# A retention layer and two feed-forward layers on one core: a new order for the opening, and every later step planned anew

## The chip, the cores and the metric

The kernel runs on one core of one Trainium2 chip. A core has a matrix engine (TensorE, "PE" in the profile; its weight loads are "PEld"), a vector engine (VectorE, "DVE"), a scalar engine (ScalarE, "ACT"), a general engine (GpSimd, "POOL") and a queue engine that here only starts transfers (SyncE, "SP"). Each engine works through its own instructions in the order in which they were written and waits on semaphores for the others. The metric is the device time of one execution in microseconds (us); lower is better.

## What is computed

The inputs are float32 for q, k and v (2 batches, 8 heads, 768 steps, 64 features a head) and 64-bit for the four weight matrices.

```python
for t in range(S):                       # retention, gamma = 1 - 2**(-5-h) by head
    state = gamma * state + einsum('bhd,bhe->bhde', k[:, :, t], v[:, :, t])
    y[:, :, t] = scale * einsum('bhd,bhde->bhe', q[:, :, t], state)
x = y as (1536 tokens, 512)
h = x @ moe_w_in                         # 512 -> 2048
g = where(h > 0, h, exp(min(h, 0)) - 1)  # ELU
x = g @ moe_w_out                        # 2048 -> 512
h = x @ moe2_w_in
g = max(h, 0) + log1p(exp(-abs(h)))      # softplus
out = g @ moe2_w_out
```

## The kernel before

**Steps.** The work is cut into some 1,950 small steps, each with a short name and up to three numbers. A table of such names, written out in the kernel (`TABLE`), is walked through from left to right once, while the program is built; each step appends its few instructions to the engines' queues. So the table alone sets the order of every engine's instructions and of the transfers. Tiles and PSUM banks are handed out in the same order, and an instruction waits until the last user of its tile is done.

**Retention.** The 1536 tokens are 12 chunks of 128, `j` = 0 to 11 (0 to 5 are the first batch, 6 to 11 the second). A chunk needs its transfers `Lq.j`, `Lk.j`, `Lv.j` (line 180 up to chunk 5, lines 183 to 188 after; from chunk 8 on q and k come in a second, blocked form by eight steps `Lb`, four small transfers each, line 204), one table of decay factors for each batch (`Lg.0`, `Lg.1`, line 771), transposes on TensorE (`Tq`, `Tk`, line 370) and their copies out of PSUM (`tq` on DVE, `tk` on ACT, lines 387 to 391; from chunk 8 on both are transposes on DVE, line 377), the scores (`S`, PE line 437), their causal mask (`m`, DVE line 447), the state (`dv` on POOL, line 363; `ST` on PE, line 417; `st` on DVE, lines 426 to 429; `sp` on POOL, line 402), and the product with the values (`O`, PE lines 459 to 480). The result, the layer's x, is split into two tiles whose sum carries the precision: the rounded part (`xh`, ACT line 495) and the rest (`xl`, DVE line 499).

**First feed-forward layer.** It goes over 48 units, `u` = 0 to 47: 3 blocks of 512 tokens (four chunks) by 16 slices of 128 of the 2048 hidden features. `H.u` is the hidden product (12 matmuls, PE line 517), `ar`, `ae` (ACT lines 525, 528) and `ab` (DVE line 532) are the ELU, `gh` (ACT line 536) and `gl` (DVE line 541) its two halves, `R.u` is the product that returns to 512 features (12 matmuls, PE line 558). `ih`, `il` and `oh`, `ol` split the weight slices of the unit in the same way (ACT line 300, DVE line 306). Unit 0 needs chunks 0 to 3. The hidden product's PSUM bank is one of two in turn, and in the second batch the state product `ST` borrows the one that is free.

**Weights.** `Lw.i` loads one weight slice of 512 KB (line 269); numbers 0 to 31 are the first layer's, 32 to 63 the second's. There are four buffers, and a fifth while the retention lasts. Four steps turn the 64-bit numbers of a slice into float32: `ct.i` and `cl.i` on ACT (lines 274, 279), `cj.i` and `cs.i` on DVE (lines 284, 293); `cs` frees the buffer.

**Second feed-forward layer.** After `R.47` the second layer runs on the finished tokens (`M`, PE line 696; `Q`, PE line 751), with its own splits (`bh`, `bl`, `sh`, `sl`, `wh`, `wl`); the finished sums of the first layer leave PSUM in steps `F` (ACT line 585, DVE line 587), and `u.0` to `u.2` are copies of partial sums that the products wait for (ACT line 703).

**What sets the order.** All q, k, v and weight transfers are issued from SP in the table's order, on one queue. `kc` are matmuls on zeros ahead of and between the first real ones.

```python
    for t in TABLE.split():
        name, *args = t.split(".")
        steps[name](*map(int, args))
```

Of the kernel before, what the change touches and what calls it, by code (L numbers as in the profile page):

```python
# [27 lines left out]
ct.3 cs.2 cl.3 cj.3 S.4 ar.0 Lw.7 cs.3 ih.2 H.1 ae.0 il.2 Lw.8 oh.0 m.4 ct.4 dv.5 cl.4 ab.0 ol.0 Tq.5 gh.0 O.4 cj.4 Lq.7
ar.1 gl.0 ae.1 cs.4 ct.5 H.2 cl.5 ab.1 ih.3 tq.5 xh.4 il.3 gh.1 cj.5 Lb.64 ct.6 xl.4 R.0 cl.6 cs.5 ar.2 gl.1 Lw.9 ct.7 oh.1
cj.6 ae.2 ol.1 H.3 cl.7 Lw.11 cs.6 ct.8 ab.2 ih.4 cj.7 cl.8 Lb.65 il.4 gh.2 cs.7 Tk.5 ST.4 ar.3 gl.2 Lk.6 tk.5 R.1 cj.8 oh.2  # L30
st.4 ct.9 Lw.10 cl.9 ol.2 sp.5 Lw.14 ae.3 cj.9 Lv.6 ct.11 ab.3 S.5 cs.9 gh.3 Lk.7 cs.8 oh.3 H.4 gl.3 ih.5 ol.3 cl.11 Lw.12
m.5 ct.10 cl.10 R.2 il.5 Lw.13 ar.4 cj.10 ae.4 cj.11 dv.6 cs.10 ab.4 Lb.66 ih.6 R.3 cs.11 gh.4 il.6 oh.4 Lw.16 gl.4 Lw.15
# [20 lines left out]
st.10 gl.24 H.25 oh.24 ol.24 R.23 ar.25 ih.27 ae.25 il.27 ab.25 H.26 gh.25 oh.25 gl.25 ol.25 R.24 ar.26 ih.28 ae.26 il.28
ab.26 H.27 gh.26 oh.26 gl.26 ol.26 S.11 ar.27 ih.29 R.25 ae.27 il.29 m.11 ab.27 H.28 gh.27 oh.27 gl.27 ol.27 O.11 end yh.0.0
ar.28 yl.0.0 ih.30 ae.28 il.30 yh.0.1 ab.28 R.26 xh.11 yl.0.1 gh.28 xl.11 gl.28 H.29 oh.28 ol.28 R.27 ar.29 ih.31 ae.29
il.31 ab.29 H.30 gh.29 oh.29 gl.29 ol.29 R.28 ar.30 ih.32 ae.30 il.32 ab.30 cs.32 H.31 gh.30 oh.30 Lw.36 gl.30 cl.34 ol.30
cj.34 R.29 ar.31 ih.33 ae.31 il.33 ab.31 ct.36 cs.33 H.32 gh.31 oh.31 cw.0.0 Lw.37 gl.31 cl.35 ol.31 cw.0.1 cw.0.2 R.30
# [773 lines left out]
```

## Time and profile before

| | |
|---|---|
| median of 3 runs | 584.48 us (583.4 to 585.72) |
| the profiled execution's own time | 584.83 us |
| its span, first to last instruction | 583.1 us |
| mean granted TensorE clock | 0.993 |
| busy: PE, PEld, DVE, ACT, POOL | 570.0, 485.5, 451.5, 371.7, 28.4 us |
| HBM traffic | 44.58 MB read, 3.15 MB written |

The span is what the trace covers; 1.73 us of the execution's own time lie around it. "Busy" counts an engine's computing instructions only. TensorE's granted clock is 1.0 at 2.4 GHz and 0.5 at 1.2 GHz.

### The profile page before, as it was taken

The numbers are of one execution on the slowest core, as the hardware profiler recorded it, in microseconds if no ns is written. First come the engines' busy times: TensorE is split into PE (matmuls) and PEld (weight loads), VectorE is DVE, ScalarE is ACT, GpSimd is POOL, SyncE is SP. The second block draws the span as 40 slices with busy tenths as digits, with TensorE's granted clock in tenths as the row PEclk, the third lists the DMA queues.
The fourth block names the chain that finished last, engine by engine and source line by source line (L and its number), as shares of the span: only waits on it lengthen the run. The fifth ranks groups of instructions, "written<-read, shape, count | busy, mean of one in ns | idle before, by whom it ended". The sixth has DMA issues, their size and how long they took to land.

```text
span 583.1 us, 8690 instructions
## 1 busy us (share of the span) xinstructions
PE 570.0 (98%) x3236; PEld 485.5 (83%) x3236; DVE 451.5 (77%) x785; ACT 371.7 (64%) x678; POOL 28.4 (5%) x37
## 2 busy tenths in 40 slices
PE   8899999999979999999999999999999999999997
PEld 5788888888857888888888899889999989998995
DVE  4799899976465465999999899877788876666653
ACT  2488988845544555888999785555567655555442
POOL 3312102101010000000000000000000000000000
PEclk9999999999979999999999999999999999999999
DMA  9998687523510000314677000000000200000002
GB/s 200 245 311 212 183 264 206 143 43 60 161 38 1 2 1 36 104 42 150 210 239 232 2 0 1 1 1 2 0 1 0 110 2 0 2 0 1 0 1 108
DMA packets 75833, 48.28 MB, mean 83 GB/s; under 512 B 53520, under 2 KB 69904, under 8 KB 75792
## 3 DMA queue, kind: packets, MB, share of 16 engines
q1 hardware_dynamic: 75504, 47.46, 29.5%
q8 instruction: 25, 0.41, 0.3%
q10 hardware_dynamic: 288, 0.28, 0.1%
q14 instruction: 16, 0.13, 0.1%
HBM read 44.58 MB, written 3.15 MB: 82 GB/s over the span
## 4 chain that ended last, share of the span: by engine, by line
PE 91%; SPq 3%; DMA 3%; ACT 1%; DVE 1%; issue 0%; DVEq 0%; ACTq 0%
PE psb L517 23%; PE psb L751 22%; PE psb L558 22%; PE psb L696 20%; DMA raw<-moe_w_in 3%; SPq L180 2%; PE psb L437 1%; SPq L269 1%; PE psb L466 1%; PE psb L370 0%; PE psb L417 0%; PE psb L459 0%; PE psb L480 0%; DMA out_dram<-o 0%; PE psb L474 0%
## 5 line engine op out<-in xcount | busy, mean ns | idle before, releaser
L751 PE MATMUL psb<-wo,g 128*128 128x512 f32 x576 | 142.1, 392 | 0.0
L751 PEld LDWEIGHTS psb<-wo,g 128*128 128x128 f32 x576 | 107.5, 188 | 19.5
L517 PE MATMUL psb<-x,wh 128*128 128x512 f32 x384 | 97.8, 397 | 5.6 <-DVE st L428 3.6
L517 PEld LDWEIGHTS psb<-x,wh 128*128 128x128 f32 x384 | 72.4, 191 | 22.0 <-ACT gh L536 4.0
L696 PE MATMUL psb<-op,wx 128*128 128x384 f32 x336 | 67.0, 339 | 0.0
L696 PEld LDWEIGHTS psb<-op,wx 128*128 128x128 f32 x336 | 60.2, 188 | 2.5
L306 DVE TENSOR_TENSOR wl<-wi,wh 128x512 fp32r<-128x512 f32 x48 | 33.7, 701 | 33.6 <-ACT wh L300 33.6
L721 ACT ACTIVATE hx<-hx 128x384 f32<-128x384 f32 x64 | 33.2, 520 | 37.5 <-DVE hx L717 37.4
L558 PE MATMUL psb<-gh,wh 128*128 128x512 f32 x192 | 56.4, 400 | 0.0
L558 PE MATMUL psb<-gh,wl 128*128 128x512 f32 x192 | 54.4, 390 | 0.0
L558 PE MATMUL psb<-gl,wh 128*128 128x512 f32 x192 | 54.3, 389 | 0.0
L517 PE MATMUL psb<-x,wl 128*128 128x512 f32 x192 | 52.2, 394 | 0.0
L284 DVE SCALAR_TENSOR_TENSOR cl<-cm,cl 128x512 int32<-128x512 int32 x64 | 45.2, 710 | 8.4 <-ACT cl L279 8.4
L274 ACT ACTIVATE cm<-raw 128x512 f32<-128x512 f32 x64 | 42.8, 668 | 12.0 <-DMA raw<-moe_w_in 8.0
L525 ACT ACTIVATE e<-psb 128x512 f32<-128x512 f32 x48 | 28.4, 592 | 34.4 <-PE psb L517 34.3
L536 ACT ACTIVATE gh<-e 128x512 fp32r<-128x512 f32 x48 | 30.2, 629 | 24.3 <-DVE e L532 24.3
L731 ACT ACTIVATE g<-hx 128x384 fp32r<-128x384 f32 x64 | 33.2, 520 | 18.7 <-DVE hx L725 18.6
L669 DVE TENSOR_TENSOR wo<-wo,wo 128x512 fp32r<-128x512 f32 x32 | 22.0, 687 | 29.7 <-ACT wo L665 29.7
L517 PEld LDWEIGHTS psb<-x,wl 128*128 128x128 f32 x192 | 36.6, 191 | 7.8
L279 ACT ACTIVATE cl<-raw 128x512 int32<-128x512 uint32 x64 | 42.5, 665 | 0.6 <-DVE wo L293 0.5
L558 PEld LDWEIGHTS psb<-gh,wl 128*128 128x128 f32 x192 | 36.1, 188 | 7.7
L558 PEld LDWEIGHTS psb<-gl,wh 128*128 128x128 f32 x192 | 36.0, 188 | 7.5
(102 smaller groups left out, 890.9 us busy)
## 6 DMA issues: line engine op xcount, KB each, us to landing
raw<-moe_w_in SPq DMA_DIRECT2D x32, 512.0 KB, 4.8
raw<-moe_w_out SPq DMA_DIRECT2D x32, 512.0 KB, 4.3
out_dram<-o SPq DMA_DIRECT2D x11, 256.0 KB, 2.2
early<-q SPq DMA_DIRECT2D x4, 256.0 KB, 5.0
early<-k SPq DMA_DIRECT2D x4, 256.0 KB, 4.9
early_v<-v SPq DMA_DIRECT2D x4, 256.0 KB, 5.3
qb<-q SPq DMA_DIRECT2D x64, 16.0 KB, 2.0
qb<-k SPq DMA_DIRECT2D x64, 16.0 KB, 1.8
```

The costliest lines, as they stand in the source:

```text
L274: nc.scalar.activation(out=m, in_=raws[i][:, :, :, 1].bitcast(F32), func=AF.Copy, scale=2.0 ** -112)
L279: nc.scalar.activation(out=l, in_=raws[i][:, :, :, 0].bitcast(U32), func=AF.Copy, scale=2.0 ** -29 * (1 - 2.0 ** -12), bias=-0.499)
L284: nc.vector.scalar_tensor_tensor(out=l, in0=m.bitcast(I32), scalar=3, in1=l, op0=ALU.logical_shift_left, op1=ALU.bitwise_or)
L306: nc.vector.tensor_tensor(out=l, in0=wf[f][o], in1=ws[u, o][0].bitcast(F32), op=ALU.subtract)
L517: nc.tensor.matmul(b, w[:, kk, :], x[:, kk, :], start=(n == 0), stop=(n == len(seq) - 1))
L525: nc.scalar.activation(out=e, in_=hb[u], func=AF.Relu, scale=-1.0)
L536: nc.scalar.activation(out=gh, in_=acts[u], func=AF.Copy)
L558: nc.tensor.matmul(acc[i], st[:, i * P:(i + 1) * P], mv, start=(fresh and p == 0), stop=(f == NF - 1 and p == 2))
L696: nc.tensor.matmul(bank_p[b], w[:, h, k], x[l][:, k], start=(start and i == 0), stop=(i == len(seq) - 1), skip_group_check=True)
L721: nc.scalar.activation(out=e, in_=e, func=AF.Softplus)
L731: nc.scalar.activation(out=t[:, 0], in_=hid[Q, c][1], func=AF.Copy)
L751: nc.tensor.matmul(sums2[s], t[:, x, i * P:(i + 1) * P], o[:, w], start=(left[s] == 0 and p == 0), stop=(left[s] == 2 * NQ - 1 and p == 2) ...
```

## The change

The table is replaced, and nothing else. Both tables hold the same steps, each exactly once. Up to `R.0`, the first product that returns to 512 features, the order is now one written out by hand; everything after it comes from a new run of the planner that made the old table, with measured times for the issue of transfers in its costs.

```diff
 TABLE = """
 ST.5 ST.11 sp.7 st.5 sp.6 sp.8 Tq.8 Tk.8 sp.9 Tq.9 Tk.9 sp.10 Tq.10 Tk.10 sp.11 Tq.11 Tk.11 st.11 Lq.0 Lk.0 Lk.1 Lq.1 Lv.0
-Lv.1 Lk.2 Lq.3 Lq.2 dq.0 Tq.0 kc.3 Lg.0 tq.0 Tk.0 Lv.2 Tk.1 tk.0 tk.1 S.0 Lk.3 dq.1 Lv.3 Tq.1 dv.0 m.0 kc.2 ST.0 Lw.0 dv.1
...
+Lg.0 Lv.1 Lk.2 dq.0 Lq.3 Tq.0 kc.3 Lq.2 tq.0 Tk.0 Lv.2 Tk.1 tk.0 tk.1 S.0 Lw.0 dq.1 Lk.3 Tq.1 dv.0 kc.2 tq.1 Lk.4 m.0 ST.0
...
```

TensorE's order is the same to the last step. Of the steps on SP, ACT, DVE and POOL, 57 of 130, 259 of 676, 225 of 764 and 8 of 21 stand at another place in their engine's queue. Three places matter below.

The first is ScalarE's queue in the opening, after `tk.2`. Before, it reads `xh.1 tk.3 ct.0 cl.0 xh.2 ih.0 tk.4 ct.1 cl.1 ct.2 cl.2 xh.3` (line 495 is `xh`, 387 `tk`, 274 and 279 a weight slice's `ct` and `cl`, 300 `ih`):

```order
L495 ACTIVATE x_234<-psb 128x4x128
L387 ACTIVATE early_v<-psb 128x512
L274 ACTIVATE cm<-raw 128x512
L279 ACTIVATE cl<-raw 128x512
L495 ACTIVATE x_234<-psb 128x4x128
L300 ACTIVATE wh<-wi_116 128x512
L387 ACTIVATE kT<-psb 128x512
L274 ACTIVATE cm<-raw 128x512
L279 ACTIVATE cl<-raw 128x512
L274 ACTIVATE cm<-raw 128x512
L279 ACTIVATE cl<-raw 128x512
L495 ACTIVATE x_234<-psb 128x4x128
```

Now the same stretch of the queue reads `ct.0 cl.0 xh.1 tk.3 xh.2 ih.0 ct.1 cl.1 xh.3 tk.4 ih.1 ct.2`:

```order
L274 ACTIVATE cm<-raw 128x512
L279 ACTIVATE cl<-raw 128x512
L495 ACTIVATE x_235<-psb 128x4x128
L387 ACTIVATE early_v<-psb 128x512
L495 ACTIVATE x_235<-psb 128x4x128
L300 ACTIVATE wh<-wi_116 128x512
L274 ACTIVATE cm<-raw 128x512
L279 ACTIVATE cl<-raw 128x512
L495 ACTIVATE x_235<-psb 128x4x128
L387 ACTIVATE kT<-psb 128x512
L300 ACTIVATE wh<-wi_116 128x512
L274 ACTIVATE cm<-raw 128x512
```

`xh.3`, the last line 495 of each, moved ahead of `ct.2`; `ct.0` moved ahead of `xh.1`. Beside it, DVE has `tq.1` ahead of `m.0` and `m.3` ahead of `xl.2` now, POOL has `sp.1` ahead of `dv.1` and `sp.3` ahead of `dv.3`, and SP issues `Lg.0` four transfers earlier (ahead of `Lv.1`), `Lw.0` ahead of `Lk.3` and `Lv.3`, and `Lw.3` and `Lw.4` ahead of `Lv.4`.

The second place is SP's queue at the end of the retention's transfers. Before, the first four weight slices of the second layer stand behind the last blocked transfers (line 204) and ahead of `Lv.11` (lines 183 to 186, v) and `Lk.11` (k):

```order
L204 DMA qb<-k 32x4x32 x16
L269 DMA raw<-moe_w_in 128x4x256 x4
L183 DMA v<-v 128x4x64
L185 DMA v<-v 64x4x64
L186 DMA v<-v 64x4x64
L183 DMA k<-k 128x4x64
L185 DMA k<-k 64x4x64
L186 DMA k<-k 64x4x64
```

Now:

```order
L204 DMA qb<-k 32x4x32 x16
L183 DMA v<-v 128x4x64
L185 DMA v<-v 64x4x64
L186 DMA v<-v 64x4x64
L269 DMA raw<-moe_w_in 128x4x256 x2
L183 DMA k<-k 128x4x64
L185 DMA k<-k 64x4x64
L186 DMA k<-k 64x4x64
L269 DMA raw<-moe_w_in 128x4x256 x2
```

`Lw.32` and `Lw.33` moved behind `Lv.11`, `Lw.34` and `Lw.35` behind `Lk.11` too.

The third place is ScalarE's queue where these four slices are taken up. Before, from `ar.19` on (lines 525, 528 and 536 are the ELU of a unit):

```order
L525 ACTIVATE e<-psb 128x512
L300 ACTIVATE wh<-wi_118 128x512
L528 ACTIVATE e<-e 128x512
L274 ACTIVATE cm<-raw 128x512
L279 ACTIVATE cl<-raw 128x512
L274 ACTIVATE cm<-raw 128x512
L279 ACTIVATE cl<-raw 128x512
L300 ACTIVATE wh<-wo_127 128x512
L536 ACTIVATE gh<-e 128x512
L274 ACTIVATE cm<-raw 128x512 x2
L525 ACTIVATE e<-psb 128x512
```

Now `ar.19` is followed by `ih.21 ae.19 gh.19 oh.19 ar.20` and no line 274; the four `ct` stand two units later. From `oh.21` on:

```order
L300 ACTIVATE wh<-wo_129 128x512
L274 ACTIVATE cm<-raw 128x512
L279 ACTIVATE cl<-raw 128x512
L274 ACTIVATE cm<-raw 128x512
L279 ACTIVATE cl<-raw 128x512
L525 ACTIVATE e<-psb 128x512
L300 ACTIVATE wh<-wi_120 128x512
L528 ACTIVATE e<-e 128x512
L274 ACTIVATE cm<-raw 128x512
L300 ACTIVATE wh<-wo_130 128x512
L536 ACTIVATE gh<-e 128x512
L274 ACTIVATE cm<-raw 128x512
```

`ct.32` moved from the middle of unit 19's ELU to behind unit 21's.

At the passage from the first layer to the second the last conversions come later: on ACT `cl.62`, `ct.63` and `cl.63` now stand behind `u.0`, and on DVE `cj.61`, `cs.61`, `cj.62` and `cs.62` behind `gl.47`; before, only `cj.63` and `cs.63` did.

## Rows read from the trace of the kernel before

**Rows 1.** Groups by line: busy, mean ns | idle before them, what ended it.

```profile
L517 PE MATMUL psb<-x,wh 128*128 128x512 f32 x384 | 97.8, 397 | 5.6 <-DVE st L428 3.6 <-ACT x L495 1.9
```

**Rows 2.** Busy time by engine in stretches of the span, with granted clock and DMA.

```profile
0.00:20.00 20.00, 17.50 (x188) 12.76 (x188) 10.81 (x20) 4.87 (x7) 8.21 (x19) 1.00 1.06 209
20.00:40.00 20.00, 17.31 (x158) 14.16 (x157) 16.91 (x28) 14.15 (x25) 4.51 (x6) 1.00 1.06 288
...
160.00:180.00 20.00, 16.38 (x60) 12.99 (x59) 11.43 (x17) 9.64 (x18) 2.45 (x2) 0.83 0.13 29
```

**Rows 3.** The same view of three short stretches around the long stall.

```profile
162.38:166.00 3.62, 0.00 (x1) 0.03 (x1) 2.33 (x5) 3.27 (x7) 0.38 (x1) 0.89 0.35 79
166.00:171.46 5.46, 5.46 (x13) 4.30 (x14) 3.83 (x4) 0.11 (x1) 2.08 (x2) 0.50 0.00 0
171.46:174.50 3.04, 3.04 (x13) 2.49 (x13) 1.29 (x2) 2.17 (x4) 0.00 (x0) 0.91 0.00 0
```

**Rows 4.** Timeline, 145 to 176 us: start, duration, instruction, [idle before it <-releaser].

```profile
144.78 7.49 SPq L204 DMA_DIRECT2D qb<-k  x16
...
152.36 2.04 SPq L269 DMA_DIRECT2D raw<-moe_w_in  x4
...
156.70 0.66 ACT L274 ACTIVATE cm<-raw 128x512 f32<-128x512 f32 x1 [4.26 <-DMA raw<-moe_w_in]
...
159.51 0.37 SPq L183 DMA_DIRECT2D v<-v  x1
...
161.93 0.66 ACT L274 ACTIVATE cm<-raw 128x512 f32<-128x512 f32 x1 [0.86 <-DMA raw<-moe_w_in]
162.50 0.58 ACT L525 ACTIVATE e<-psb 128x512 f32<-128x512 f32 x1
...
166.00 3.75 PE L517 MATMUL psb<-x,wh 128*128 128x512 f32 x8 [3.62 <-DVE st L428]
```

**Rows 5.** Timeline of the opening, 18 to 30 us.

```profile
18.39 1.04 POOL L363 TENSOR_TENSOR early_v<-early_v,dec 128x512 f32<-128x512 f32 x1 [0.66 <-DMA early_v<-v]
...
18.70 0.66 PE L370 MATMUL psb<-ident,early 128*128 128x128 f32 x4
...
20.50 0.67 ACT L274 ACTIVATE cm<-raw 128x512 f32<-128x512 f32 x1 [0.51 <-DMA raw<-moe_w_in]
...
21.20 1.16 PE L437 MATMUL psb<-early_v 64*128 64x128 f32 x16
...
23.70 1.28 DVE L447 TENSOR_TENSOR A<-psb,mask 128x512 f32<-128x512 f32 x2
...
25.04 0.98 PE L480 MATMUL psb<-A,early_v 128*64 128x128 f32 x13 [0.17 <-DVE A L447]
...
26.52 0.66 PE L370 MATMUL psb<-ident,q 128*128 128x128 f32 x4
...
27.36 0.66 ACT L274 ACTIVATE cm<-raw 128x512 f32<-128x512 f32 x1 [1.66 <-DMA raw<-moe_w_in]
...
28.47 0.59 ACT L495 ACTIVATE x<-psb 128x512 fp32r<-128x512 f32 x1
...
29.11 1.20 PE L517 MATMUL psb<-x,wh 128*128 128x512 f32 x4 [1.93 <-ACT x L495]
```

**Rows 6.** Timeline of VectorE and TensorE, 119 to 124 us.

```profile
119.09 0.64 DVE L306 TENSOR_TENSOR wl<-wi,wh 128x512 fp32r<-128x512 f32 x1
...
122.47 1.98 PE L517 MATMUL psb<-x,wh 128*128 128x512 f32 x8
```

**Rows 7.** Timeline at the passage to the second layer, 326 to 334 us.

```profile
326.20 1.06 ACT L647 ACTIVATE wx<-wi 128x1024 fp32r<-128x1024 f32 x1 [1.36 <-DVE wi L637]
...
329.14 0.56 DVE L725 SCALAR_TENSOR_TENSOR hx<-hx 128x384 f32<-128x384 f32 x1 [0.61 <-ACT hx L721]
...
330.53 1.04 ACT L585 ACTIVATE y<-psb 128x384 f32<-128x384 f32 x2 [1.05 <-DVE y L587]
...
333.19 0.29 DVE L587 COPY y<-psb 128x128 f32<-128x128 f32 x1 [1.46 <-PE psb L558]
```

More of the change, by code (lines that the diff above doesn't have):

```diff
@@ L28 @@
[L28 to L32, printed above, removed]
@@ L53 @@
[L53 to L57, printed above, removed]
@@ L115 @@
[L115 to L117 removed]
+Lg.0 Lv.1 Lk.2 dq.0 Lq.3 Tq.0 kc.3 Lq.2 tq.0 Tk.0 Lv.2 Tk.1 tk.0 tk.1 S.0 Lw.0 dq.1 Lk.3 Tq.1 dv.0 kc.2 tq.1 Lk.4 m.0 ST.0
+Lv.3 st.0 O.0 sp.1 Lw.1 S.1 xh.0 dv.1 Lq.4 xl.0 Tk.2 m.1 ST.1 tk.2 Lw.2 Tq.3 Tq.2 st.1 O.1 Lw.3 dv.2 tq.2 tq.3 sp.2 S.2 Lw.4
@@ new lines @@
+H.21 oh.20 Lw.33 Lk.11 ol.20 R.19 Lw.34 dv.11 ar.21 Lw.35 ih.23 ae.21 il.23 ab.21 H.22 gh.21 oh.21 gl.21 ct.32 ol.21 cl.32
+ct.33 cj.32 R.20 cl.33 ar.22 cj.33 ih.24 ae.22 il.24 ab.22 ct.34 H.23 oh.22 gh.22 ol.22 ct.35 gl.22 S.10 ar.23 ih.25 R.21
+ae.23 il.25 m.10 ab.23 H.24 gh.23 oh.23 gl.23 ol.23 O.10 ar.24 ih.26 ae.24 il.26 ab.24 ST.10 xh.10 gh.24 R.22 xl.10 st.10
+gl.24 H.25 oh.24 ol.24 R.23 ar.25 ih.27 ae.25 il.27 ab.25 H.26 gh.25 oh.25 gl.25 ol.25 R.24 ar.26 ih.28 ae.26 il.28 ab.26
+H.27 gh.26 oh.26 gl.26 ol.26 S.11 ar.27 ih.29 R.25 ae.27 il.29 m.11 ab.27 H.28 gh.27 oh.27 gl.27 ol.27 O.11 end yh.0.0 ar.28
@@ new lines @@
+Q.0.0 j.0.3 vh.0.2 j.0.1 wh.2 c.1.0 vh.0.3 wl.1 vh.0.1 M.1.6 yh.1.0 vl.0.2 vl.0.1 yh.1.1 M.1.5 cw.2.0 cw.2.1 u.1 cw.2.2
+Q.0.1 vl.0.3 bh.2 n.1.0 wl.2 s.1.0 bl.2 M.1.7 wh.3 j.1.0 Q.0.2 cw.2.3 u.2 wl.3 vh.1.0 sh.2 c.1.2 vl.1.0 M.1.4 n.1.2 sl.2
+s.1.2 M.1.3 j.1.2 c.1.3 cw.3.0 vh.1.2 n.1.3 Q.0.3 cw.3.1 s.1.3 c.1.1 j.1.3 n.1.1 vh.1.3 vl.1.2 M.2.1 s.1.1 cw.3.2 wh.4
+vl.1.3 j.1.1 bh.3 M.2.2 wl.4 u.0 Q.1.0 bl.3 vh.1.1 c.2.0 vl.1.1 M.2.6 n.2.0 cw.3.3 s.2.0 yl.1.0 sh.3 M.2.5 j.2.0 u.1 sl.3
+Q.1.1 vh.2.0 vl.2.0 cw.4.0 cw.4.1 cw.4.2 M.2.7 wh.5 yl.1.1 Q.1.2 wl.5 u.2 cw.4.3 c.2.2 xt.1.0 M.2.4 n.2.2 xt.1.2 s.2.2 M.2.3
@@ new lines @@
+u.0 vh.9.1 vl.9.3 Q.9.0 c.10.0 vl.9.1 n.10.0 sl.11 s.10.0 M.10.6 j.10.0 cw.12.1 vh.10.0 M.10.5 cw.12.0 u.1 vl.10.0 Q.9.1
+M.10.7 wh.21 wl.21 Q.9.2 u.2 c.10.2 n.10.2 s.10.2 M.10.4 j.10.2 M.10.3 vh.10.2 c.10.3 vl.10.2 bh.12 Q.9.3 n.10.3 c.10.1
+s.10.3 n.10.1 bl.12 sh.12 s.10.1 M.11.1 j.10.3 wh.22 j.10.1 vh.10.3 M.11.2 wl.22 u.0 vh.10.1 vl.10.3 Q.10.0 c.11.0 vl.10.1
+n.11.0 sl.12 s.11.0 M.11.6 j.11.0 cw.13.1 vh.11.0 M.11.5 cw.13.0 u.1 vl.11.0 Q.10.1 M.11.7 wh.23 wl.23 Q.10.2 u.2 c.11.2
+n.11.2 s.11.2 M.11.4 j.11.2 M.11.3 vh.11.2 c.11.3 vl.11.2 bh.13 Q.10.3 n.11.3 c.11.1 s.11.3 n.11.1 bl.13 sh.13 s.11.1 M.12.1
@@ L118 @@
+n.15.1 j.15.3 s.15.1 vh.15.3 j.15.1 Q.15.0 vl.15.3 vh.15.1 vl.15.1 Q.15.2 Q.15.3 Q.15.1 o.1.1 o.1.0 o.1.2 d.1.0 d.1.1 d.1.2
+o.1.3 d.1.3 o.1.4 d.1.4 o.1.5 d.1.5
 """
```

158 lines of the change are left out of this document (75 added, 83 removed).

## The prediction

> **What bounds the kernel now.** I read the groups by line first, for the product that opens each unit, then the busy time by stretches, then the timelines around the stretches where TensorE is not full. TensorE's own work is untouched by the change: its order is the same to the last step, so only what it waits for can move. The hidden product's 384 matmuls stood idle 5.6 us in all, and two waits make that up: 3.6 us for a step of the state on VectorE and 1.9 us for x on ScalarE [rows 1]. By stretches TensorE is short of full in the first 40 us (17.50 and 17.31 of 20) and around 160 to 180 us (16.38, at a mean granted clock of 0.83) [rows 2]. The two waits lie in the second and third of these.
>
> The long one runs from 162.38 to 166.00 us, and it costs more than its length [rows 3]. `H.21` and `R.19`, 24 matmuls, follow it. The first 12 take 5.46 us at a granted clock of 0.50 (1.2 GHz) and the other 12 take 3.04 us; twelve at the full clock take 2.72 us, which is half of 5.46 to 0.01. So the stall is worth 3.62 idle, 2.74 and 0.32 of slow clock: **6.68 us**.
>
> Where it comes from stands in the timeline [rows 4]. SP needs 7.49 us for 16 small blocked transfers, 0.47 us each, and so starts `Lw.32` to `Lw.35` only at 152.36. ScalarE stands at `ct.32`, in the middle of unit 19's ELU, for 4.26 us until 156.70, and once more until `Lw.35` has landed (161.93). Only then, at 162.50, does it reach `ar.20`, the first step of the next unit's ELU. VectorE's `ab.20`, its transpose for chunk 11 and `st.9` queue behind that, and `st.9` holds the PSUM bank that `H.21` needs.
>
> The short wait is in the opening [rows 5]. TensorE has done `Tq.4` at 27.18 (26.52 and 0.66) and stands until 29.11 for `xh.3`. The product that `xh.3` copies, `O.3`, ended at 26.02 (25.04 and 0.98). But ScalarE's queue had `ct.2` first, which waited 1.66 us for `Lw.2`, began at 27.36, and let `xh.3` begin at 28.47.
>
> **The change, part by part.** *The long stall.* The four `ct` now stand behind `oh.21`, and the loads behind `Lv.11` and `Lk.11`. `Lv.11` takes the buffers of chunk 9, so SP cannot start it before `ST.9` is done: SP stood from 154.40 (152.36 and 2.04) to 159.51 for that [rows 4]. With the opening's 1.93 us (below) taken off, that is 157.6. Its three issues at 0.47 end at 159.0, so `Lw.32` lands at 159.0 and the 4.34 us that it took before (152.36 to 156.70): 163.3. `Lw.35` follows two weight issues and three more for `Lk.11`; the four loads landed 1.74 us apart before ((161.93 - 156.70)/3), three of these gaps and 0.8 us for `Lk.11`, an estimate at under half of a load, give 169.4. ScalarE needs them when unit 21's ELU is through: `R.18` ends at 162.38 - 1.93 = 160.45, `H.21` 2.72 us later at 163.2, and six steps in a chain at 0.58 to 0.66 us [rows 4, 6] bring it to `ct.32` at 167.0 and to `ct.35`, behind the next unit's `ar` and `ae`, at about 171. The loads are there 3.7 and 1.6 us ahead, and what stands behind a late `ct.35`, the ELU of unit 23, has most of a unit (two products, 5.44 us) in hand. I take the whole **-6.68 us**; the bounds are nothing, if ScalarE meets the same wait in a later unit, and 6.68.
>
> The Trainium skill speaks against this part: "DMA: Bandwidth & Descriptors", section "Issuing engines are not separate DMA queues", has it that the time to start a transfer is usually small beside the transfer. The trace does not agree for these: 16 issues held SP for 7.49 us [rows 4]. By the page a plan that counts issue times has nothing to gain here, and the sum would keep the 6.68 us.
>
> The Trainium skill's "TensorE: Matmul & The Clock Gate", section "Terms", puts the price of a slow clock at the throttled time by the share of the clock that is missing. The clocks of rows 3 make 6.8 us at 0.50, so 3.4 us by that rule; the matmuls show 2.74 and 0.32, 3.06 us, since part of the slow time falls on an idle engine. The sum by the rule would be 0.3 us lower.
>
> *The opening, from `xh.3` on.* With `ct.2` behind it, `xh.3` follows `O.3` at once, and `ct.1`, which stands ahead of it, finds `Lw.1` landed two transfers before `Lw.2`. The end of `O.3` at 26.02 and 0.59 for `xh.3` is 26.6, under `Tq.4`'s end at 27.18: `H.0` starts then, **-1.93 us**. Had TensorE nothing between `O.3` and `H.0`, `xh.3` itself would be 2.42 us earlier (28.47 - 26.05), which bounds the gain.
>
> *The opening, ahead of `O.3`.* Two moves cost something there. `tq.1` ahead of `m.0` puts the mask one step later on VectorE, 0.64 us (1.28/2 [rows 5]), and TensorE's `O.0`, `S.1`, `O.1`, `S.2` with it, 0.5 us as there was little room. `Lw.0` ahead of `Lk.3` delays that by one weight load, 2.11 us (20.50 - 18.39, behind `Lv.3`). `Lk.3` stood one transfer ahead of `Lv.3`; an estimate of half a load's time between them puts it at 17.3 before and 19.4 now, so `Tk.3` moves from 18.70 to 19.5 at the least, `S.3` from 21.20 to about 22.3, ending at 23.5. But before, `m.3` began only at 23.70, 1.3 us after `S.3` had ended (21.20 and 1.16), for it stood behind `xl.2` and two conversions; now it stands ahead of `xl.2` and begins at 23.5 to 23.7. So `O.3` ends where it did: **0**, bounds -0.2 and +1.0. What is late next if `S.3` slips further is `m.3` one for one. `dv.3`, whose `Lv.3` now lands behind `Lw.0` and `Lk.4` (2.11 and, by the same estimate, 1.05), begins at 21.6 instead of 18.39, or at about 23 behind `sp.3`, ends by 24.1 and is hidden behind `m.3`, whose second half ends at 24.9; without that cover it would cost its own 1.04. The same for `ct.0` ahead of `xh.1`: it ties `xh.1`, `xl.1`, `st.2` and `sp.3` to `Lw.0`, and `m.3` covers them up to a landing of about 19.5 (I expect 18.4 to 18.7, two transfers ahead of the 20.50 of before).
>
> *The long middle.* TensorE arrives 1.93 us earlier at every unit, and the other engines must keep up. The smallest lead that I find of a split weight on its product is `H.15`'s, 119.73 (119.09 and 0.64) against 122.47: 2.7 us, and that half is wanted only in the product's last third [rows 6]. The new plan has the conversions there one step later on both engines, with fewer ahead of each split. I take **0**, bounds 0 and +1.
>
> *The passage to the second layer.* Three conversions more on ScalarE, 0.56 us apart, 1.7 us, meet idle times of 1.36 and 1.05; four more on VectorE, 0.6 apart, 2.4 us, meet 0.61 and 1.46 that are shown [rows 7]. I take **+0.3**; with the cover gone it would be 2.4 on VectorE, where `F.47` and the partial sum behind it (333.19) would come late and `M.0.3` after them.
>
> Sum against the profiled execution's own 584.83: - 6.68 - 1.93 + 0 + 0 + 0.30 = 576.52. The median of the runs is 0.35 lower (584.48), so **576.2 us**.
>
> **Rivals.** *The stall stays.* The loads are not started earlier than before (159.0 against 152.36), so if ScalarE still meets them unlanded, two units on, the same queue stands behind it. For it: the four loads still come last on SP and need up to 9.6 us to land (152.36 to 161.93). Against: 3.7 us of room. Only the opening is gained then: 582.9, or 584 with the opening lost too; I take 582 to 586. It is also what the Trainium skill's rule on issue times, above, would give. *The opening gives nothing.* `Lk.3`, `ct.0` and `dv.3` are all tied to `Lw.0`; if it lands later than 19.5, `O.3` and `H.0` slip one for one. At 21.4 the gain is gone: 578.1, up to 581 with the passage's whole cost. *Slower.* The place is SP at `Lv.11`: whatever delays `ST.9` or the blocked transfers ahead now delays all four weight loads too, which before did not wait for it. From a landing of `Lw.35` past some 176 us (171 and most of a unit) each us costs one, and an idle TensorE costs the 3.06 us of slow clock again. To be slower than 587.4 it must land past 176 + 8.2 + 2.9 - 3.1 = 184, 15 us later than I expect; SP had nothing of that size in it before.
>
> **How the numbers follow.** Half a per cent, 2.9 us, is about what a measurement of this kernel can tell from no change. My forecast holds with 0.70, between 574.5 and 578; the opening without gain has 0.12 (578 to 581); the stall that stays 0.09 (582 to 586); slower 0.05; better than 574.5, by a wait that I have not seen, 0.04. Faster: 0.70 + 0.12 + 0.04 = 0.86; same 0.09; slower 0.05. Range 574.5 to 580.5: forecast and most of the second case, about 0.8.
>
> **What would show it.** In the profile after: the groups by line of the hidden product with hardly any idle time behind VectorE and ScalarE; a granted clock of 1.0 from 160 to 180 us; `H.0` at 27.2; `ct.32` without a wait; `M.0.3` no more than 0.3 us later against `R.47`. Wrong would be a new wait of ScalarE or VectorE for a transfer between 40 and 180 us, or a `Tk.3` past 20 us.

## The result

| | before | changed |
|---|---|---|
| median of the timed runs | 585.1 us (four runs, 583.4 to 586.14) | **579.33 us** (four runs, 578.8 to 580.23) |
| the profiled execution's own time, span | 584.83, 583.1 | 578.8, 576.7 |
| mean granted clock | 0.993 | 1.000 |

The ratio is 0.9906, with a 95 % interval of 0.9877 to 0.9934: faster by 0.9 %, as forecast in sign, and 3.1 us short of the forecast 576.2. The page's groups by line and the busy time by stretches answer to [rows 1] and [rows 2]:

```profile
L517 PE MATMUL psb<-x,wh 128*128 128x512 f32 x384 | 96.0, 392 | 1.2 <-DVE st L428 1.2
...
L558 PE MATMUL psb<-gh,wl 128*128 128x512 f32 x192 | 54.5, 390 | 0.8 <-DVE wl L306 0.8
```

```profile
core 0: us, PE busy (x) PEld busy (x) DVE busy (x) ACT busy (x) POOL busy (x), PEclk, DMA share, GB/s
0.00:20.00 20.00, 17.45 (x176) 12.31 (x176) 9.31 (x16) 5.28 (x8) 7.16 (x18) 1.00 1.09 211
20.00:40.00 20.00, 19.60 (x177) 16.33 (x173) 19.65 (x33) 15.34 (x28) 5.85 (x7) 1.00 1.02 283
160.00:180.00 20.00, 20.00 (x100) 16.35 (x99) 13.38 (x22) 11.74 (x22) 2.40 (x2) 1.00 0.50 132
```

The two waits of the hidden product of [rows 1], 3.6 and 1.9 us, are gone, and TensorE is full from 160 to 180 us at the full clock. But two shorter waits stand there that the kernel before did not have: 1.2 us for another step of the state (line 428) and 0.8 us for a low half of weights (line 306).

TensorE's order is the same in both kernels, so the time can be followed from step to step in its timeline. Each row is the time from the start of one TensorE step to the start of another:

| from, to | before | changed | difference |
|---|---|---|---|
| start of the span, `Tq.1` | 8.60 | 9.43 | +0.83 |
| `Tq.1`, `H.0` | 20.51 | 17.57 | -2.94 |
| `H.0`, `R.0` | 12.21 | 12.20 | -0.01 |
| `R.0`, `H.3` | 2.72 | 3.87 | **+1.15** |
| `H.3`, `R.9` | 59.26 | 59.21 | -0.05 |
| `R.9`, `H.13` | 8.29 | 9.81 | **+1.52** |
| `H.13`, `H.18` | 30.85 | 30.65 | -0.20 |
| `H.18`, `H.22` | 31.89 | 25.21 | **-6.68** |
| `H.22`, `H.46` | 137.00 | 137.00 | 0 |

In all 6.37 us less up to `H.46` (311.34 and 304.97), which is the difference of the spans, 6.4. The first two rows belong together: `Tq.1` comes at a different time in each execution, and in the order of before a later `Tq.1` is made up again ahead of `Tq.4` by shorter waits, for POOL's values at `ST.0` and for the masks at `O.3` (17.92 us from `Tq.1` to `Tq.4` with `Tq.1` at 8.60; 17.12 with `Tq.1` at 9.06, in the run with the opening's three moves below). So the opening gave their sum, 2.11 us. The two new waits cost more than that: at `H.13` the changed kernel is 0.51 us behind the kernel before (112.10 and 111.59). What is left at the end comes from the long stall.

The long stall's place, TensorE and then ScalarE, for [rows 3, 4]:

```profile
162.53 1.98 PE L517 MATMUL psb<-x,wh 128*128 128x512 f32 x8
164.34 1.07 PE L517 MATMUL psb<-x,wl 128*128 128x512 f32 x4
165.25 1.07 PE L558 MATMUL psb<-gh,wh 128*128 128x512 f32 x4
...
167.97 1.98 PE L517 MATMUL psb<-x,wh 128*128 128x512 f32 x8
```

```profile
168.46 0.62 ACT L300 ACTIVATE wh<-wo 128x512 fp32r<-128x512 f32 x1
168.98 0.66 ACT L274 ACTIVATE cm<-raw 128x512 f32<-128x512 f32 x1
...
174.66 0.66 ACT L274 ACTIVATE cm<-raw 128x512 f32<-128x512 f32 x1
```

`H.21` follows without a gap, and the 24 matmuls up to `H.22` take 5.44 us (162.53 to 167.97) where they took 8.34 (166.00 to 174.34). `ct.32` (168.98) and `ct.35` (174.66) show no idle time in brackets: the loads are there, the first since 166.34 and the last since 172.31.

The first new wait is `R.0`'s, in TensorE's timeline; VectorE's shows why:

```profile
39.20 0.40 PE L558 MATMUL psb<-gh,wh 128*128 128x512 f32 x1
40.45 0.51 PE L558 MATMUL psb<-gh,wl 128*128 128x512 f32 x1 [0.85 <-DVE wl L306]
```

```profile
37.31 0.68 DVE L306 TENSOR_TENSOR wl<-wi,wh 128x512 fp32r<-128x512 f32 x1
37.91 0.68 DVE L532 SCALAR_TENSOR_TENSOR e<-e,psb 128x512 f32<-128x512 f32 x1
38.51 0.68 DVE L541 TENSOR_TENSOR gl<-e,gh 128x512 fp32r<-128x512 f32 x1
39.11 0.68 DVE L499 TENSOR_TENSOR x<-psb,x 128x512 fp32r<-128x512 f32 x1
39.71 0.68 DVE L306 TENSOR_TENSOR wl<-wo,wh 128x512 fp32r<-128x512 f32 x1
```

`R.0` opens a block, so it finishes one slice of the output after the other and wants the low half `ol.0` for its second matmul. `ol.0` (`wl<-wo`) now stands behind `il.2`, `ab.1`, `gl.0` and `xl.4` and is ready at 40.39; before it was ready at 37.43. The second new wait is `H.12`'s:

```profile
104.23 1.07 PE L558 MATMUL psb<-gl,wh 128*128 128x512 f32 x4
106.54 2.09 PE L517 MATMUL psb<-x,wh 128*128 128x512 f32 x8 [1.24 <-DVE st L428]
```

```profile
104.78 0.68 DVE L532 SCALAR_TENSOR_TENSOR e<-e,psb 128x512 f32<-128x512 f32 x1
105.38 0.68 DVE L293 SCALAR_TENSOR_TENSOR wo<-raw,cl 128x512 int32<-128x512 int32 x1
105.98 0.42 DVE L428 TENSOR_TENSOR st<-psb,st 128x256 f32<-128x256 f32 x1
```

The state's product `ST.7` ended at 102.36, but `st.7`, which frees its PSUM bank for `H.12`, stands behind `ab.11` and a conversion (`cs.25`) and begins 3.6 us later. In the kernel before there was little to spare here as well: `st.7` freed the bank at 105.90, 0.25 us ahead of `H.12` (106.15).

### The profile page after: what moved, and what is told of

Its sections match the earlier page's. It is cut to its first block, busy times and chain, and to the rows that moved or that the text cites. A ratio compares the mean times of both kernels' runs of the same rounds, so it can differ in the third digit from the quotient of the medians.

```text
span 576.7 us, 8692 instructions
## 1 busy us (share of the span) xinstructions
PE 567.8 (98%) x3236; PEld 484.1 (84%) x3236; DVE 451.6 (78%) x785; ACT 372.4 (65%) x678; POOL 27.2 (5%) x37
## 4 chain that ended last, share of the span: by engine, by line
PE 91%; DVE 5%; DMA 2%; issue 1%; ACT 0%; DVEq 0%
PE psb L751 22%; PE psb L558 22%; PE psb L696 21%; PE psb L517 20%; PE psb L437 2%; PE psb L370 1%; DVE cl L284 1%; DVE A L447 1%; PE psb L480 1%; PE psb L417 1%; DMA raw<-moe_w_out 1%; DVE wi L293 1%; DVE wl L306 1%; DMA early<-q 1%; PE psb L466 1%
## 5 line engine op out<-in xcount | busy, mean ns | idle before, releaser
L751 PEld LDWEIGHTS psb<-wo,g 128*128 128x128 f32 x576 | 107.5, 188 | 19.4
L517 PE MATMUL psb<-x,wh 128*128 128x512 f32 x384 | 96.0, 392 | 1.2 <-DVE st L428 1.2
L306 DVE TENSOR_TENSOR wl<-wi,wh 128x512 fp32r<-128x512 f32 x48 | 35.4, 738 | 33.1 <-ACT wh L300 32.8
```

The costliest lines, as they stand in the source:

```text
L306: nc.vector.tensor_tensor(out=l, in0=wf[f][o], in1=ws[u, o][0].bitcast(F32), op=ALU.subtract)
L517: nc.tensor.matmul(b, w[:, kk, :], x[:, kk, :], start=(n == 0), stop=(n == len(seq) - 1))
L751: nc.tensor.matmul(sums2[s], t[:, x, i * P:(i + 1) * P], o[:, w], start=(left[s] == 0 and p == 0), stop=(left[s] == 2 * NQ - 1 and p == 2) ...
```

## The experiments

All of them change only the table and leave out no step; the last one adds two warm-up matmuls. The steps' starts are read as in the table above. A ratio compares with the kernel before on the same chip; where only "the profiled execution" is given, it is the only one.

**The long stall: ScalarE's queue or the transfers?**

```diff
-... il.21 ct.32 m.9 cl.32 ab.19 ct.33 tk.11 cl.33 H.20 oh.19 cj.32 gh.19 cj.33 ct.34 ol.19 gl.19 O.9 ct.35 ar.20
+... il.21 m.9 ab.19 tk.11 H.20 oh.19 gh.19 ol.19 gl.19 O.9 ar.20
...
-gh.21 oh.21 gl.21 ol.21 R.20 ar.22 ih.24 ae.22 il.24 ab.22 H.23 gh.22 oh.22 gl.22
+gh.21 oh.21 gl.21 ct.32 ol.21 cl.32 ct.33 cj.32 R.20 cl.33 ar.22 cj.33 ih.24 ae.22 il.24 ab.22 ct.34 H.23 gh.22 oh.22 ct.35 gl.22
```

> The kernel before with ct.32 to ct.35 and their cl.32, cl.33, cj.32, cj.33 alone moved to where the change has them, behind unit 21's ELU; SP's order, and with it every transfer, is that of before. Theory (the long stall is a matter of ScalarE's queue alone): H.21 starts without its 3.62 us of idle time and H.21 and R.19 run at a granted clock of 1.0, so TensorE is 6.7 us earlier from H.22 on; span 583.1 - 6.7 = 576.4, measured time about 578. Rival (the order of transfers with their issue times is what removes it): a stall of 3 us or more remains at H.21 or moves to H.23, span 580 or more.

Measured 578.97 us against 585.5 on that chip, ratio 0.9884 (0.9851 to 0.9917). From `H.18` to `H.22` 25.21 us, the changed kernel's own figure to 0.01, where the kernel before has 31.89: the whole 6.68 us come from the place of these conversions in ScalarE's queue (and of their `cj` in VectorE's), with SP's order untouched. The theory holds, the rival falls. The span was 579.1 and not 576.4, for two reasons ahead of the stall. `H.0`'s short wait was followed by a slow clock in this execution (told at the end), 1.59 us. And `H.13` to `H.18` took 31.95 instead of 30.85, with a wait for `st.8` at `H.17` that the profile of the kernel before does not show.

**The opening: is it `xh.3` alone?**

```diff
-ct.2 cs.1 cl.2 few ST.3 xh.3 Lw.6
+xh.3 ct.2 cs.1 cl.2 few ST.3 Lw.6
```

> The kernel before with xh.3 alone moved ahead of ct.2 and cl.2 on ScalarE. Theory: H.0 starts 1.9 to 2.1 us earlier, at 27.0 to 27.2, and R.0 keeps all of it (its ol.0 stands early in that order). What is left of it later depends on what the later waits hang on: if the long stall's end is set by the loads and not by TensorE, it grows by what was gained, H.22 starts at 174.3 as before and the span stays at 583; if not, 581. I expect the first, within 1 us. Rival (the opening's other moves are what made H.0 earlier): H.0 within 0.5 us of 29.11.

The profiled execution took 584.86 us, span 583.1. `H.0` starts 0.41 us after `Tq.4` instead of 2.59, but the gain is given back at once:

```profile
27.96 1.17 PE L517 MATMUL psb<-x,wh 128*128 128x512 f32 x4
28.97 1.08 PE L517 MATMUL psb<-x,wl 128*128 128x512 f32 x4
30.36 1.20 PE L517 MATMUL psb<-x,wh 128*128 128x512 f32 x4 [0.31 <-DVE x L499]
31.75 1.16 PE L437 MATMUL psb<-qT,kT 64*128 64x128 f32 x16 [0.20 <-DVE qT L391]
...
36.53 0.66 PE L370 MATMUL psb<-ident,q 128*128 128x128 f32 x4 [0.69 <-DVE A L447]
```

`xl.3` (line 499) and then the masks `m.4` (line 447) are late on VectorE, and `Tq.4` to `R.0` takes 14.63 us, against 14.80 before and 12.61 in the changed kernel. So the theory that one move carries the opening falls: 0.17 us are left of 2.18. The rest of this expectation was not put to the test, since TensorE came to `H.18` later and not earlier (144.00 against 142.45). The stall was still there, 3.27 us with a slow clock behind it.

The two moves together:

> The kernel before with both single moves: xh.3 ahead of ct.2, and ct.32 to ct.35 with cl.32, cl.33, cj.32, cj.33 behind unit 21's ELU. Nothing else of the change. Theory: both gains add, 6.7 and 1.0 to 2.1 us; span 574.3 to 575.4, 1.3 to 2.4 us under the changed kernel's 576.7, since the new waits at R.0 and H.12 are not in this order. Rival (the changed order of the transfers carries part of the gain): span 577 or more.

580.13 us, ratio 0.9923 (0.9894 to 0.9952), span 578.4: the two gains do not add, and the span lies where the rival had put it. The rival's reason, the order of the transfers, is settled further down, by a run that keeps SP's order of before. `Tq.4` to `R.0` took 15.48, 0.68 more than before; `H.18` to `H.22` 25.21. `H.13` to `H.18` again cost 1.2 us more than before, 32.09.

**What else the opening needs.** To the two moves were added two on VectorE, `cj.2` behind `il.1` and `m.4` ahead of `cj.3`:

```diff
-cj.2 ih.1 xl.3 Tq.4 st.3 H.0 tq.4 sp.4 il.1 Lq.6 ct.3 cs.2 cl.3 cj.3 S.4 ar.0
+ih.1 xl.3 Tq.4 st.3 H.0 tq.4 sp.4 il.1 Lq.6 ct.3 cj.2 cs.2 cl.3 S.4 m.4 cj.3 ar.0
```

> The kernel before with xh.3 ahead of ct.2, ct.32 to cj.33 behind unit 21's ELU, and two more moves on VectorE in the opening: cj.2 behind il.1 (so xl.3 no longer stands behind it), and m.4 ahead of cj.3. Theory: with xh.3 moved alone H.0 came earlier and the gain was given back at once, 1.15 us to xl.3 and 1.0 us to the masks m.4, both behind conversions on VectorE; with these two moves R.0 keeps 2 us against Tq.4 (15.0 to 12.8 us from Tq.4 to R.0). H.17 may still wait for st.8 behind the blocked k transfers, about 1 us. Rival: ScalarE's or the loads' own lateness holds H.1 or R.0, and Tq.4 to R.0 stays over 14 us.

The profiled execution took 578.73 us, span 577.0. `Tq.4` to `R.0` 12.59: three moves make the opening's gain from `Tq.4` on, 2.21 us, and the changed kernel has no more of it. But now TensorE comes to `H.13` 2.4 us earlier than in the kernel before (109.19 and 111.59), and stands at `H.17`. First TensorE, then VectorE:

```profile
133.50 1.07 PE L558 MATMUL psb<-gl,wh 128*128 128x512 f32 x4
137.50 2.06 PE L517 MATMUL psb<-x,wh 128*128 128x512 f32 x8 [2.93 <-DVE st L428]
```

```profile
133.94 0.71 DVE L377 STREAM_TRANSPOSE kT<-qb 128x512 f32<-128x512 f32 x1 [5.33 <-DMA qb<-k]
134.58 0.65 DVE L306 TENSOR_TENSOR wl<-wi,wh 128x512 fp32r<-128x512 f32 x1
135.15 0.68 DVE L532 SCALAR_TENSOR_TENSOR e<-e,psb 128x512 f32<-128x512 f32 x1
135.75 0.70 DVE L377 STREAM_TRANSPOSE qT<-qb 128x512 f32<-128x512 f32 x1
136.37 0.65 DVE L499 TENSOR_TENSOR x<-psb,x 128x512 fp32r<-128x512 f32 x1
136.95 0.40 DVE L428 TENSOR_TENSOR st<-psb,st 128x256 f32<-128x256 f32 x1
```

`tk.10` waits for the blocked transfers of `k`, and `st.8`, five steps behind it, holds the bank. `H.13` to `H.18` takes 33.83 us: 2.98 of the gains are eaten here. In the kernel before the same place was close to a wait; SP, VectorE and TensorE there:

```profile
124.39 7.73 SPq L204 DMA_DIRECT2D qb<-k  x16
...
133.37 0.71 DVE L377 STREAM_TRANSPOSE kT<-qb 128x512 f32<-128x512 f32 x1 [2.35 <-DMA qb<-k]
...
136.37 0.41 DVE L428 TENSOR_TENSOR st<-psb,st 128x256 f32<-128x256 f32 x1
...
136.92 2.06 PE L517 MATMUL psb<-x,wh 128*128 128x512 f32 x8
```

`tk.10` already waited 2.35 us there, and `st.8` freed the bank at 136.78, 0.14 us ahead of `H.17`. So it does not take an early TensorE: in the first three runs above (the late conversions, `xh.3`, and both) `H.17` waits 0.66 to 1.15 us although TensorE comes to `H.13` 0.5 to 1.5 us later than in the kernel before, for SP starts these 16 transfers 1.4 to 2.6 us later (125.80 to 126.98). What delays SP there stays open.

The new plan has `tk.10` one unit later. Is its place the cause of the wait?

```diff
-ar.16 ih.18 tk.10 ae.16 il.18 Lb.89 ab.16
+ar.16 ih.18 ae.16 il.18 Lb.89 ab.16
...
-ar.17 ih.19 ae.17 il.19 Lb.92 ab.17 H.18
+ar.17 ih.19 ae.17 il.19 Lb.92 ab.17 tk.10 H.18
```

> As the kernel with the opening's three moves and the late conversions, and besides tk.10, VectorE's transpose of chunk 10's k, behind ab.17 instead of ahead of ab.16. Theory: H.17's wait of about 1.1 us in the runs that kept the old order there comes from tk.10, which waits up to 3.5 us for 16 blocked transfers at 0.47 us of issue each and holds st.8 back; with tk.10 later H.17 starts without a wait, and the kernel comes to 575 to 577 us, no slower than the changed one. Rival: the blocked k or v transfers hold another step there (tq.10, dv.10), and a wait of 1 us or more at H.17 to H.19 stays.

577.8 us, ratio 0.9899 (0.9866 to 0.9932), span 575.1. `H.13` to `H.18` 30.65, the changed kernel's figure: the wait came from `tk.10`'s place. The order of before with these few moves is level with the changed kernel, whose ratio is 0.9906. SP's order is that of before, so the rival of the two moves falls: the order of the transfers is not needed for the gain. (A wait of 0.68 us for `st.7` at `H.12` appears here too, with `st.7` at its old place.) The counter-test, in the changed kernel `tk.10` alone put back, with the table's entries of its loads:

```diff
-ar.16 ih.18 Lb.84 ae.16 il.18 ab.16 ST.8 Lb.85
+ar.16 ih.18 Lb.84 Lb.85 Lb.86 Lb.87 tk.10 ae.16 il.18 ab.16 ST.8
```

> The changed kernel with tk.10 alone put back to its place in the kernel before on VectorE, ahead of il.18 and ab.16; SP's order unchanged. Theory: tk.10 waits for the last of 16 blocked k transfers, which SP issues until 137.9 us in the changed kernel, holds ab.16, tq.10, xl.8 and st.8 back, and H.17 starts at 140 to 142 instead of 137.3, 3 to 5 us later (a little more if the clock falls); span 580 to 582. So the new plan's place of tk.10 would be worth as much as the opening, which the profile of the kernel before does not show. Rival: the transfers land soon enough, H.17 moves by under 1 us, span 577.

The profiled execution took 586.65 us, span 584.9, more than the kernel before.

```profile
139.68 0.71 DVE L377 STREAM_TRANSPOSE kT<-qb 128x512 f32<-128x512 f32 x1 [8.77 <-DMA qb<-k]
```

```profile
143.23 3.75 PE L517 MATMUL psb<-x,wh 128*128 128x512 f32 x8 [6.37 <-DVE st L428]
146.78 1.59 PE L517 MATMUL psb<-x,wl 128*128 128x512 f32 x4
```

```profile
122.00 7.72 SPq L204 DMA_DIRECT2D qb<-q  x16
129.76 8.66 SPq L204 DMA_DIRECT2D qb<-k  x16
```

`H.17` stands for 6.37 us, and the granted clock is 0.60 from 140 to 145 us and 0.71 from 145 to 150; `H.13` to `H.18` takes 39.45, 8.80 more. The mechanism held and its price was put too low, by the slow clock and the later landing. The SP queue (the last view) says why: 32 blocked transfers in a row, 16.4 us of issues. The price is that of this transfer order: in the changed kernel SP starts the 16 transfers of `k` at 129.44, 5 us later than in the kernel before (124.39), so `tk.10`'s old place costs 8.80 here and cost 2.98 in the order of before.

**The two new waits.** In the changed kernel, first `oh.0`, `ol.0` and `gl.0` alone:

```diff
-ae.1 tq.5 gh.0 Lq.7 cs.4 ct.5 il.2 cl.5 xh.4 Lw.9 ab.1 H.2 oh.0 gl.0 ih.3 xl.4 gh.1 ol.0 ct.6
+ae.1 tq.5 gh.0 oh.0 Lq.7 cs.4 ct.5 il.2 ol.0 gl.0 cl.5 xh.4 Lw.9 ab.1 H.2 ih.3 xl.4 gh.1 ct.6
```

> The changed kernel with only the first of its two new waits removed: oh.0 directly behind gh.0 on ScalarE, ol.0 and gl.0 directly behind il.2 on VectorE. Theory: R.0 takes 2.9 us instead of 4.03, and H.12 still waits for st.7 about as long as in the changed kernel (1.24 us), since VectorE follows TensorE again at 62 us; H.0 to the end 1.1 to 1.2 us less than in the changed kernel. Rival (VectorE's queue is full from 40 to 110 us and does not come earlier): st.7 stays where it is, H.12 waits some 2.4 us, and nothing is left behind it.

`R.0` to `H.3` 2.72, `R.9` to `H.12` still 4.14 (4.25 in the changed kernel), and from `Tq.1` to `H.46` 294.30 us against 295.53: 1.23 gained and kept. (Span 576.7 and time 578.8 us, no less than the changed kernel's, since this execution reached `Tq.1` only at 10.61; more on that at the end.) Then `ST.7` and `st.7` alone:

```diff
-O.7 cl.25 cs.24 Lw.28 ar.11 ol.10 Lw.29 ih.13 cj.25 ae.11 il.13 ct.26 ST.7 ab.11 cl.26 Lb.74 cs.25 ct.27 R.9 st.7
+O.7 ST.7 st.7 cl.25 cs.24 Lw.28 ar.11 ol.10 Lw.29 ih.13 cj.25 ae.11 il.13 ct.26 ab.11 cl.26 Lb.74 cs.25 ct.27 R.9
```

> The changed kernel with only the second of its two new waits removed: ST.7 and st.7 directly behind O.7. Theory: R.0 still takes 3.87 us up to H.3, H.12 starts without its 1.24 us, R.9 to H.12 takes 2.85 us instead of 4.25, so 1.4 us are gained from there to the end and the two waits add up (1.15 and 1.4). Rival: another step of VectorE's queue, delayed by st.7, makes a later product wait, and the gain is under 0.7 us.

576.94 us in the one execution; `R.9` to `H.12` 2.85 instead of 4.25, `R.0` to `H.3` still 3.99. From `Tq.1` to `H.46` 294.41, 1.12 less; the 1.40 at `H.12` is there, and 0.28 was lost ahead of `R.0`, where nothing was changed (the second execution of the changed kernel, below, loses 0.26 there). Both together:

> The changed kernel with its two new waits removed: oh.0 directly behind gh.0 on ScalarE with ol.0 and gl.0 directly behind il.2 on VectorE, and ST.7 and st.7 directly behind O.7. Theory (the changed kernel lost 1.15 us at R.0 and 1.5 at H.12, both to the place of one step in VectorE's queue): R.0 takes 2.9 us instead of 4.03, H.12 starts without its 1.24 us, TensorE is 2.4 to 2.7 us earlier from H.13 to the end; span 576.7 - 2.5 = 574.2. Rival (VectorE is full from 40 to 110 us, so its queue and not one step's place sets the time): the waits appear at the next product, and the span stays at 576 or more.

576.34 us, ratio 0.9846 (0.9818 to 0.9874), span 575.2. `R.0` and `H.12` show no idle time, and `Tq.1` to `H.46` takes 292.86: 2.67 us less than in the changed kernel, as forecast (the span shows 1.5 of them, since `Tq.1` came at 10.53 against 9.43). The rival, that VectorE's full queue sets the time, falls: the places of `ol.0` and `st.7` (with `oh.0`, `gl.0` and `ST.7`, which go with them) did.

**A version faster than the changed kernel.** With `m.0` ahead of `tq.1` as well, as the kernel before has it:

```diff
-kc.2 tq.1 Lk.4 m.0 ST.0
+kc.2 m.0 tq.1 Lk.4 ST.0
```

> As the kernel with both new waits removed (oh.0, ol.0, gl.0 and ST.7, st.7 moved), and besides m.0 ahead of tq.1 on VectorE, as in the kernel before. In the changed kernel TensorE has no idle time from O.0 to R.0 except O.0's own wait for the mask. Theory: O.0 starts without its 0.33 and 0.16 us of waiting, and as TensorE is full behind it, H.0 and all that follows comes 0.5 us earlier against Tq.1 than in the kernel with both waits removed: from Tq.1 to H.0 17.1 us instead of 17.57, about 574 to 576 us measured. Rival: S.1 then waits for tq.1, or O.3 for m.3, and Tq.1 to H.0 stays at 17.5.

**575.39 us**, ratio 0.9862 (0.9826 to 0.9898), span 573.4. This is the lowest time, but on another chip than the run before it, whose ratio is 0.9846: by the ratios the two cannot be told apart. `Tq.1` to `H.46` takes 292.62, 0.24 us less, which is about what two executions of one kernel differ by (0.21, below). So most of the gain over the changed kernel is that of the two waits, and what `m.0` adds is not shown. `O.0` has no wait, but two come behind it:

```profile
13.57 0.69 PE L417 MATMUL psb<-early_v,early 128*64 128x64 f32 x16 [0.28 <-POOL early_v L363]
...
19.26 0.66 PE L370 MATMUL psb<-ident,early 128*128 128x128 f32 x4 [0.35 <-DMA early<-k]
```

They are for `dv.1`, now behind `sp.1`, and for `Lk.3`, now behind `Lw.0`. `Tq.1` to `H.0` is 17.28 instead of 17.57, where 17.1 was expected.

**How much differs from one execution to the next.** The changed kernel once more, and the best version with two more warm-up matmuls ahead of `Tq.0`:

> The changed kernel itself, unaltered, on the same chip and beside the same runs of the kernel before as the kernel with the warm-up matmuls. Theory: 578.5 to 579.5 us, 3 to 4 us over the kernel with the two waits removed and m.0 first; Tq.1 to H.46 takes 295.5 us as before, and only the stretch ahead of Tq.1 differs between executions. Rival: R.0's and H.12's waits vary from one execution to the next, and Tq.1 to H.46 differs by over 0.5 us.

578.46 us against 583.15 on that chip, ratio 0.9914 (0.9885 to 0.9943). `Tq.1` to `H.46` 295.74 (295.53 the first time), with 3.98 from `R.0` to `H.3` and 4.04 from `R.9` to `H.12` (3.87 and 4.25): the two waits are there in both profiled executions of the changed kernel.

```diff
-dq.0 Lq.3 Tq.0
+dq.0 kc.2 Tq.0 Lq.3
```

> As the kernel with both new waits removed and m.0 ahead of tq.1, and besides two more warm-up matmuls (kc.2) ahead of Tq.0. In every run so far the stretch from Tq.0 to Tq.1 took between 3.59 and 5.55 us with the same work in it, and its three warm matmuls between 0.81 and 1.49 us, while the profile records a granted clock of 1.0. Theory: the slow pace follows the idle time of 0.33 to 0.80 us ahead of Tq.0; with that filled Tq.0 to Tq.1 takes 3.6 to 3.9 us and the runs lie closer together, 0.5 to 1 us lower in the median. Rival: the pace does not hang on that idle time (one run with 0.35 us was fast, one with 0.33 slow), and Tq.0 to Tq.1 stays at 4.2 or more, or the added matmuls delay Tq.0 by what they gain.

575.62 us on the same chip as the run above, 2.8 us under it, and no better than without the two matmuls (575.39). `Tq.0` begins without a wait, and `Tq.0` to `Tq.1` still takes 4.24 us (4.26 without them). The theory falls: that idle time is not what makes the stretch slow. `Tq.1` to `H.46` is 292.71, so the gain over the changed kernel, 3.0 us on this chip, is there in a second execution.

## Why the prediction came out as it did

The time, 579.33 us, lies inside the stated range, 574.5 to 580.5, and outside the forecast's own part of it, 574.5 to 578. It lies where the rival "the opening gives nothing" had been put (578 to 581), and that rival's mechanism did not come, for `H.0` began at 27.00. So the two large terms were right, and that the range held all the same is luck: the loss that filled it, 2.5 us in the long middle, has no place in the prediction beyond a bound of 1.

- **The long stall**, -6.68: measured -6.68, `H.18` to `H.22`. The mechanism was shown by moving the conversions alone. SP's new order was not needed for it; what that order is worth by itself no run shows. The rival in which the stall stays did not come. The dates were 2 to 4 us later than forecast on both sides (`Lw.35` landed at 172.31, not 169.4; `ct.35` began at 174.66, not 171), so the room at the end was 2.35 us for the 1.6 forecast.
- **The opening from `xh.3` on**, -1.93 with a start at 27.2: measured -2.11, at 27.00. The size was right, the reason incomplete: with `xh.3` alone almost nothing is left at `R.0`, and the gain needs `xl.3` and `m.4` ahead of conversions (`cj.2`, `cj.3`) on VectorE too. The new order has both; the prediction named neither.
- **The opening ahead of `O.3`**, 0: from `S.1` to `Tk.4` TensorE was 1.3 us later, and `O.3` began at 24.11 against 22.79, but the masks of `m.3` no longer made it wait, so it ended as before. 0.83 of the 1.3 lies ahead of `Tq.1`, in a stretch that varies by itself; 0.5 is `O.0`'s wait for the mask, as forecast. `Lk.3` (forecast 19.4) landed at 19.13 and is what the version with `m.0` first waits for. A `Tk.3` past 20 us was named as a sign of being wrong; it came, at 20.03, and cost nothing behind the masks. The zero does not hang on one pair of executions: where `Tq.1` came by 9.43, `Tq.4` begins at 26.17 to 26.68 in the five with the order of before in this part, and at 26.06 to 26.59 in the four with the new one.
- **The long middle**, 0 with a bound of +1: here the prediction failed. It measured **+2.47** (1.15 at `R.0`, 1.52 up to `H.13`, -0.20 up to `H.18`). The step that failed is the sentence that took the smallest lead of a split weight, `H.15`'s, for the whole test. 2.7 us was not the smallest lead: `st.7` freed its bank 0.25 us ahead of `H.12` and `st.8` 0.14 us ahead of `H.17`, and of the states that hold a PSUM bank the prediction followed only `st.9`. With `st.7` at its old place an earlier TensorE waits 0.68 us for it in one run (with `tk.10` moved) and not at all in another (the opening's three moves); the changed kernel's two executions have 1.24 and 1.03, so most of this wait is the new place's. Nor did it look at the steps that the new order puts late: it did not see that `R.0` wants its low half for its second matmul, and `ol.0`'s lead there was 4.1 us before (37.43 and 41.55). With these 2.5 us the sum would have been 578.7 for a measured 579.33. Part of `ol.0`'s lateness is likely `cj.3`, ahead of it in VectorE's queue, which took 1.50 us for the usual 0.69 while POOL multiplied the values of two chunks (31.68 to 33.73); no run without that overlap was made.

```profile
32.77 1.50 DVE L284 SCALAR_TENSOR_TENSOR cl<-cm,cl 128x512 int32<-128x512 int32 x1
```

- And the same term hid a move that mattered. Against the profile of before, `H.13` to `H.18` differs by 0.2 us; but with `tk.10` in its old place the changed kernel takes 8.8 us more there, and the order of before with an earlier TensorE takes 2.98 more. The old profile has the sign of it, VectorE's 2.35 us at `tk.10`, though no wait of TensorE. Whether the measured issue times in the planner's costs brought the new place is not shown, as there is no plan without them; the same plan also made these transfers 5 us later. The prediction had weighed the Trainium skill's "DMA: Bandwidth & Descriptors", section "Issuing engines are not separate DMA queues", by which the time to start a transfer is usually small beside the transfer. For these transfers the measurement decides against it: in the counter-test 16 of them held SP for 8.66 us, and `tk.10` began 1.26 us after the last issue (138.42 and 139.68).
- **The passage to the second layer**, +0.3: measured 0; `H.22` to `H.46` takes 137.00 in both, and the rest of the span moves along.

## What to carry to other kernels

When a gain makes the bottleneck engine arrive earlier, test the whole rest of the order against the earlier arrival: for each step that frees a bank or makes an operand, how much lead it had and when the new queue lets it start. Conversions ahead of a short step that frees a bank can become a wait of the bottleneck (1.24 us at `H.12`); here such a step could move up without a loss elsewhere. A wait that the bottleneck's old profile does not show can be a few tenths of a us away (0.14 and 0.25 here). Steps that hang on a long row of small transfers are the first to look at, and a wait of another engine at them, like VectorE's 2.35 us, is the sign.
